# A new order of all steps for a linear-attention and feed-forward kernel on one core

## The chip, the core and the metric

The kernel runs on one core of a Trainium2 chip. A core has TensorE (PE in the profile, its weight loads PEld), VectorE (DVE), ScalarE (ACT), GpSimd (POOL) and SyncE (SP), which here only issues DMA transfers. Each engine works through its own instructions in order and waits for others by semaphores. SBUF holds the operands; PSUM, in eight banks, takes what TensorE produces. The metric is the device time of the program in microseconds.

## The reference

A gated linear recurrence per head, followed by a feed-forward layer on all heads of a token:

```python
# q, k, v, f_logit: (batch 4, heads 8, seq 768, head_dim 48)
f = 1.0 / (1.0 + np.exp(-f_logit))
state = np.zeros((B, H, D, D))
for t in range(S):
    state = f[:, :, t, :, None] * state + np.einsum('bhd,bhe->bhde', k[:, :, t], v[:, :, t])
    y[:, :, t] = np.einsum('bhd,bhde->bhe', q[:, :, t], state)
x = y.transpose(0, 2, 1, 3).reshape(B * S, H * D)      # 3072 x 384
h = x @ w_in                                           # 384 x 2048
out = (h * np.cos(h)) @ w_out                          # 2048 x 384
```

## The kernel before

The 3072 tokens are cut into 12 **pairs** of 256 tokens (`pair(n)`), three for each batch entry; a pair has two chunks of 128 tokens, and the recurrence is written as products of matrices within a chunk plus a carried state. The feed-forward part (`moe(m)`) goes over 13 **units**: units 0 and 1 are the two halves of pair 0 (128 tokens each), and unit m from 2 on is pair m - 1 (256 tokens).

A **step** is a named piece of work of one engine, made of one instruction or a few. Steps of pair n, where u or g after the dot is the half of the heads or the chunk:

- `f`, `k`, `q`, `v`: loads (L296). Pairs 0 and 1 load `f`, `k` and `q` in two halves of 192 KB; the others are whole, 384 KB. `f0.0` or `f0.1` may go by ScalarE's queue.
- `ex`, `ln`, `fx`, `fy` (ScalarE, L329 to L347): the exponential, the softplus and the gate. `ad` (GpSimd, L363) adds two tokens' values. `cum` (TensorE, L374 and L380) sums along time; `eb` and `ei` (ScalarE, L391, L395) take the exponentials of the sums.
- `qa`, `ka`, `qm`, `km` (L338 to L351, L404): q and k scaled, on GpSimd, or in pairs 0 and 1 some on VectorE. `vb`, `vt`: v cast and copied, on GpSimd or ScalarE.
- `tq`, `tk` (L435): transposes on TensorE, copied out of PSUM by `qkt`; for pairs 5 to 11 ("turned") `tq` is a transposing DMA on SyncE's queue instead (L424).
- `sc` (TensorE, L456): scores; `am` (VectorE, L461): their mask. `ps` (TensorE, L479): the new state; `st` and `sz` (VectorE, L497, L503): carrying and decaying it. `y` and `yi` (TensorE, L531): the output within the chunk and from the state. `xe` (ScalarE or VectorE, L197): the output copied to SBUF as the feed-forward part's input.

Steps of unit m: `h` (TensorE, L579): a half of 1024 columns of the first product; `co` (ScalarE, L584): the cosine, by the sine function; `g` (VectorE, L561): h times the cosine. `o` (TensorE, L595, named by the block of 128 tokens): a quarter of the second product; `ot` (ScalarE or VectorE, L197): its copy; `out`: the store. `w` and `wc`: the load of a quarter of a weight matrix, and its cast (L197). All copies have line 197, since one helper writes them.

`zf` (TensorE, L264) is a product of zeros, 128 x 512, into a PSUM bank of its own choice; no result uses it. `z...` of other names clear parts of buffers once.

What sets the order: `describe` builds all steps with what they read and write, and `emit` writes them out in the order of one long string, `ORDER`. A word such as `am1.0:V2` says: step `am1.0`, on VectorE (T TensorE, S ScalarE, V VectorE, G GpSimd, Y SyncE), with its result in place 2 of its pool; where no number stands, the step writes into a value whose place is given already. So the string fixes each engine's queue, the engine of the steps that may choose, and every buffer's place, and with the places who waits for whom: a step that takes a place waits for all readers of what was there. For PSUM the places are the banks 0 to 7; `h` and `sc` take two neighbouring banks, the others one. `apart` releases two steps from each other where they use different banks of one PSUM tile.

On ScalarE the exponential and the sine need different tables; `emit` marks the changes to the first (L637), and a change costs an `ACT_TABLE_LOAD`.

Of the kernel before, what the change touches and what calls it, by code (L numbers as in the profile page):

```python
# [717 lines left out]
```

## Time and profile before

| | |
|---|---|
| time, median of 3 runs (lowest to highest) | 183.1 us (182.93 to 183.41) |
| span of the profiled execution, first to last instruction | 180.9 us |
| around the span, by the median | 2.2 us |
| granted TensorE clock, mean | 1.000 |
| TensorE's last product ends | 177.61 us |
| moved by DMA | 33.93 MB, mean 188 GB/s |

The profile shows one execution. A row of a timeline has the start and the length in us, the engine, the line, what is written and read, and how many instructions are merged in it; in brackets stands how long the engine was idle before, and what ended that. Lengths of merged rows run from the first start to the last end, and neighbouring instructions of an engine overlap by a little. TensorE's products are pipelined: the time from start to start is what a product costs in a row of them.

### The profile page before, as it was taken

To read this page: it belongs to the slowest core of one execution; us is meant where nothing else is said; L and a number is where in the kernel's file an instruction comes from. 1 tells how busy PE (TensorE), PEld (TensorE's weight loads), DVE (VectorE), ACT (ScalarE), POOL (GpSimd) and SP (SyncE) were. 2 spreads that over 40 slices of the span, in tenths; PEclk is the share of its full clock that TensorE was granted. 3 is DMA by queue.
4 is the path that set the end of the run, shared out by engine and by line. 5 is a ranking of instruction groups with operands and counts; after the bars stand their busy time and mean duration, and the time that the engine had idled before them with its cause. 6 is when DMAs were issued, how large, how long until landed. Compare 5 with 4: busy or idle time off the path is not lost.

```text
span 180.9 us, 5814 instructions
## 1 busy us (share of the span) xinstructions
PE 172.6 (95%) x2460; PEld 123.9 (69%) x2464; DVE 134.6 (74%) x206; ACT 130.7 (72%) x187; POOL 109.2 (60%) x139
## 2 busy tenths in 40 slices
...
GB/s 149 261 261 276 343 320 341 250 318 284 301 265 233 274 83 123 252 210 145 122 180 308 173 267 278 124 131 251 203 92 182 100 4 0 43 47 4 130 43 131
DMA packets 72282, 33.93 MB, mean 188 GB/s; under 512 B 65344, under 2 KB 70720, under 8 KB 72256
## 3 DMA queue, kind: packets, MB, share of 16 engines
...
## 4 chain that ended last, share of the span: by engine, by line
PE 81%; DMA 7%; ACT 3%; DVE 3%; SPq 2%; issue 1%; ACTq 0%
PE ps L595 35%; PE ps L579 33%; PE ps L531 5%; DMA f<-in_f_logit_dram 4%; PE ps L456 4%; DMA v<-in_v_dram 3%; SPq L296 2%; PE ps L479 2%; DVE g L561 1%; PE ps L435 1%; PE ps L374 1%; DVE am L461 1%; PE ps L264 1%; ACT f L344 0%; ACT f L329 0%
## 5 line engine op out<-in xcount | busy, mean ns | idle before, releaser
L561 DVE TENSOR_TENSOR g<-ps,co 128x1024 bf16<-128x1024 f32 x48 | 57.4, 1220 | 18.0 <-ACT co L584 16.7
L595 PE MATMUL ps<-w_out_bf,g 128*128 128x384 bf16 x384 | 68.9, 326 | 0.0
L579 PE MATMUL ps<-x,w_in_bf 128*128 128x256 bf16 (+1 forms) x624 | 68.1, 264 | 0.5 <-DVE x L197 0.4
L584 ACT ACTIVATE co<-ps,halfpi 128x1024 bf16<-128x1024 f32 x48 | 52.7, 1113 | 19.8 <-PE ps L579 19.5
L579 PEld LDWEIGHTS <-w_in_bf 128*128 128x128 bf16 x624 | 56.3, 98 | 9.2 <-DVE x L197 0.6
L595 PEld LDWEIGHTS <-g 128*128 128x128 bf16 x384 | 36.1, 98 | 21.4
L461 DVE TENSOR_TENSOR am<-ps,pmask 128x1024 bf16<-128x1024 f32 x24 | 28.7, 1218 | 5.2 <-PE ps L456 4.9
L404 POOL TENSOR_TENSOR qk<-k,bi 128x384 bf16<-128x384 f32 x22 | 22.0, 1008 | 5.4 <-ACT bi L391 4.7
L404 POOL TENSOR_TENSOR qk<-q,b 128x384 bf16<-128x384 f32 x21 | 20.8, 1000 | 2.7 <-DVE q L338 2.1
L197 POOL COPY vt<-vb 64x384 bf16<-64x384 bf16 x33 | 16.7, 507 | 1.6
L264 PE MATMUL ps<-zero 128*128 128x512 bf16 x50 | 14.6, 412 | 1.5 <-DVE zero L203 1.2
L503 DVE TENSOR_TENSOR sz<-ps,b 64x192 bf16<-64x192 f32 x40 | 14.1, 354 | 2.5 <-PE ps L479 1.6
L363 POOL TENSOR_TENSOR sp<-ls 128x384 bf16<-128x384 f32 x10 | 10.3, 1028 | 7.8 <-ACT ls L333 6.1
L341 POOL TENSOR_TENSOR q<-f,q 128x384 f32<-128x384 f32 x10 | 10.0, 998 | 8.0 <-DMA q<-in_q_dram 5.8
L329 ACT ACTIVATE f<-f 128x768 f32<-128x768 f32 (+1 forms) x14 | 10.4, 746 | 4.4 <-DMA f<-in_f_logit_dram 4.4
L497 DVE TENSOR_TENSOR ps<-ps,sz 64x192 f32<-64x192 f32 x32 | 11.7, 367 | 2.2 <-PE ps L479 1.1
L351 POOL TENSOR_TENSOR k<-k,f 128x384 f32<-128x384 f32 (+1 forms) x12 | 11.1, 931 | 3.4 <-DMA k<-in_k_dram 3.4
L197 ACT COPY ot<-ps 128x384 f32<-128x384 f32 (+1 forms) x14 | 6.1, 453 | 8.7 <-PE ps L595 8.7
L197 ACT CAST x<-ps 128x384 bf16<-128x384 f32 x12 | 5.5, 479 | 6.0 <-PE ps L531 6.0
L456 PE MATMUL ps<-qkt 48*64 48x128 bf16 (+1 forms) x304 | 8.7, 218 | 1.1 <-ACT x L197 0.8
L197 DVE CAST x<-ps 128x384 bf16<-128x384 f32 x12 | 6.4, 553 | 4.1 <-PE ps L531 3.9
L264 PEld LDWEIGHTS <-zero 128*128 128x128 bf16 x54 | 4.8, 103 | 5.9 <-issue 1.9
...
## 6 DMA issues: line engine op xcount, KB each, us to landing
...
```

The lines of the kernel that those rows point to most:

```text
L197: (nc.scalar.copy if e == "ACT" else eng(e).tensor_copy)(out=o, in_=i)
L264: G.step(f"zf{i}", ("PE",), lambda e, dump=dump: nc.tensor.matmul(dump.ap, lhsT=zero[:, 0:128], rhs=zero, start=True, stop=True), writes=[ ...
L351: eng(e).tensor_mul(out=w.ap[:, :, 0, :], in0=w.ap[:, :, 0, :], in1=t.ap[:, :, 0, :])
L404: G.step(f"{nm}{n}.{u}", ("POOL", "DVE") if cut else ("POOL",), lambda e, u=u, j=j, src=src, dec=dec: eng(e).tensor_mul(out=qkp[u][j].ap[: ...
L456: nc.tensor.matmul(o[t0:t1, r, 2 * a + g, :].rearrange("p (e n) -> p e n", e=2), lhsT=wide[s, t0 // 64, :] if turned else wide[s].rearrang ...
L461: G.step(f"am{n}.{u}", ("DVE",), lambda e, u=u, sc=sc: nc.vector.tensor_mul(out=am[u].ap.rearrange("p r b n -> p (r b) n"), in0=sc.ap.rear ...
L497: nc.vector.tensor_add(out=view()[s], in0=view()[s], in1=S0.ap[s, :, r, :])
L503: eng(e).tensor_mul(out=new.ap[s, :, r, :].rearrange("p (u a) n -> p u a n", u=2), in0=view()[s].rearrange("p (u a) n -> p u a n", u=2), i ...
L561: nc.vector.tensor_mul(out=o.rearrange("p b (n e) -> p b n e", e=2), in0=ph.ap.rearrange("p (b e n) -> p b n e", e=2, n=64), in1=co.ap.rea ...
L579: nc.tensor.matmul(ph.ap[:, i * T:(i + 1) * T].rearrange("p (g t) -> p g t", t=C), lhsT=w_in_bf[:, kk, f0:f0 + 128], rhs=xa[:, :, kk, :], ...
L584: G.step(f"co{m}.{j}", ("ACT",), lambda e, ph=ph, co=co: nc.scalar.activation(out=co.ap, in_=ph.ap, func=AF.Sin, bias=halfpi), reads=[ph], ...
L595: nc.tensor.matmul(po.ap[:, 0:DM], lhsT=gT.ap[:, j, i * C:(i + 1) * C], rhs=w_out_bf[:, j, :], start=(po.first and j == 4 * s), stop=(po.f ...
```

## The change

`ORDER` is replaced as a whole: all 899 steps other than the zero products stand in a new sequence; engines and places are chosen anew; and there are 58 zero products instead of 54. The steps themselves, their shapes and their number are the same, and so are the pools.

Counted over the two strings: `xe` goes from 12 on ScalarE and 12 on VectorE to 8 and 16, `ot` from 14 and 12 to 10 and 16; `vb` from 9 on GpSimd and 3 on ScalarE to 8 and 4; of the scalings of pairs 0 and 1, `qm` has one more and `km` one less on VectorE. One more of the last stores goes by ScalarE's queue. But for the clears, the other choices keep their numbers. ScalarE's queue changes between the two tables 10 times before (5 to the sine, 5 back) and 12 times after.

TensorE's first feed-forward step is `h0.01` before, between parts of pair 1; after, it is `h1.00`, behind all of pairs 0 and 1. The weights are loaded in the order `w0.1 w0.0 w0.3 w0.2 w1.0 w1.2 w1.3 w1.1` before and `w0.0 w0.2 w0.1 w0.3 w1.2 w1.1 w1.3 w1.0` after.

The beginning and the end of both strings:

```diff
 WITHIN = 12
-ZEROS = 54
+ZEROS = 58
...
 ORDER = """
-zvt.2:V zsp.1:V zsp.0:G zsz.3:V f0.1:Y0 f0.0:S zqk.0:G k0.0:Y0 ex0.1:S ex0.0:S k0.1:Y ln0.1:S1
-zf0:T0 zf1:T0 zf2:T0 zf3:T0 zf4:T0 zf5:T0 zf6:T0 zf7:T0 zf8:T0 zf9:T0 cum0.1:T0 ln0.0:S cum0.0:T1
-fx0.0:S ei0.1:S0 fx0.1:S ei0.0:S ka0.0:V f1.1:Y1 km0.0:G0 f1.0:Y ex1.1:S ka0.1:V zf10:T2 zf11:T2
-zf12:T2 zf13:T2 zf14:T2 zf15:T2 zf16:T2 zf17:T2 tk0.0:T2 eb0.1:S0 ex1.0:S ln1.1:S1 ln1.0:S fx1.0:S
-q0.1:Y0 q0.0:Y v0:Y0 fx1.1:S eb0.0:S qa0.1:V zqk.1:V qm0.1:V vb0:S0 f3:Y2 k1.1:Y1 km0.1:V qa0.0:V
-zf18:T3 cum1.1:T3 zf19:T4 zf20:T4 zf21:T4 tq0.1:T0 cum1.0:T1 qm0.0:G zsz.2:G eb1.0:S1 vt0.3:S2
-k1.0:Y ei1.0:S0 ex3:S zf22:T4 zf23:T4 zf24:T4 zf25:T4 zf26:T4 ps0.1:T4,5 ps0.0:T tk0.1:T v1:Y1 f2:Y0
-qkt0.1:V0 eb1.1:S ln3:S0 ei1.1:S ka1.0:G q1.0:Y0 tq0.0:T ka1.1:G km1.1:G0 zvt.1:G vt0.0:S ad3:G1
-vt0.1:G q1.1:Y vb1:S1 qkt0.0:V1 vt0.2:G zsz.1:G ex2:S w0.1:Y0 w0.0:Y1 k3:Y0 q3:Y1 w0.3:Y2 ln2:S1
-vt1.2:S1 fy3:S zf27:T6 zf28:T6 zf29:T6 zf30:T6 zf31:T6 zf32:T6 sc0.0:T0 sz0.01:V2 sz0.00:V w0.2:Y3
-ad2:G0 vt1.0:G km1.0:V vt1.3:G wc0.1:G am0.0:V0 zf33:T6 zf34:T6 yi0:T4 sc0.1:T2 am0.1:V1 st0.11:V
-sz0.11:V3 wc0.0:G k2:Y1 zf35:T6 zf36:T6 zf37:T6 zf38:T6 ps1.1:T6,7 tk1.0:T0 ps1.0:T zf39:T1 zf40:T1
-zf41:T1 cum3:T1 fy2:S ei3:S0 fx3:S ka3:G eb3:S2 vt1.1:S fx2:S km3.0:G1 qa3:G qm3.0:G km3.1:G qm3.1:G
-w1.0:Y0 qa1.0:V st0.10:V qa1.1:V qm1.0:V wc0.2:G ka2:G q2:Y2 tk1.1:T2 zf42:T3 zf43:T3 y0:T3 tq1.0:T
-xe0.1:S0 sz0.10:V st1.00:V st1.01:V qm1.1:V v2:Y1 zf44:T5 zf45:T5 zf46:T5 zf47:T5 zf48:T5 tq1.1:T
-cum2:T1 sz1.00:V1 qkt1.0:V0 eb2:S0 xe0.0:S ei2:S1 qkt1.1:V1 km2.0:G0 km2.1:G zf49:T5 sc1.0:T4
-sz1.01:V zf50:T0 zf51:T0 sc1.1:T2 h0.01:T0 st1.11:V sz1.11:V2 am1.1:V0 wc1.0:G qa2:G zf52:T6 zf53:T6
-h0.00:T co0.0:S0 qm2.1:G am1.0:V1 h1.01:T2 h1.00:T co1.0:S1 y1:T6,4 yi1:T g0.0:V1 xe1.1:V1 st1.10:V
-qm2.0:G vb2:G1 sz1.10:V g1.0:V4 w1.2:Y3 xe1.0:S tk3.0:T5 h2.01:T0 tq3.0:T w1.3:Y0 qkt3.0:V0 v3:Y0
-f4:Y0 h2.10:T6 h2.00:T sc3.0:T4 tq3.1:T2 tk3.1:T h2.11:T wc1.2:G wc1.3:G vt2.1:G1 wc0.3:S vb3:G0
-co2.0:S1 am3.0:V0 g2.0:V2 h2.20:T4 h2.21:T h0.11:T0 co2.1:S0 qkt3.1:S1 co2.2:S1 sc3.1:T2 w1.1:Y3
-g2.1:V am3.1:V1 g2.2:V h0.10:T h1.11:T6 h1.10:T h2.30:T2 tk2.1:T4 tk2.0:T5 co0.1:S0 co1.1:S2 g0.1:V
-g1.1:V h2.31:T o2.0:T0 co2.3:S0 tq2.1:T vt3.2:G2 vt3.1:G tq2.0:T o0.0:T1 o3.0:T6 o1.0:T7 qkt2.0:S2
...
-o22.1:T3 o22.2:T out16:Y o20.3:T6 o20.0:T g11.1:V o20.1:T h12.01:T o20.2:T co12.0:S0 g12.0:V o21.2:T
-o22.3:T o21.1:T o23.3:T7 o22.0:T ot20:V3 ot21:V1 out20:Y ot22.0:V2 ot22.1:V out22.0:Y out21:Y
-out22.1:Y o23.2:T o23.0:T o23.1:T ot23.0:S3 out23.0:Y ot23.1:S out23.1:S
+zqk.2:G k0.1:Y1 zqk.0:G zsz.0:V zvt.0:V f0.0:S1 zsp.0:V ex0.0:S f0.1:Y ex0.1:S ln0.1:S0 fx0.1:S
+ln0.0:S f1.1:Y2 ex1.1:S zf0:T0 zf1:T0 zf2:T0 zf3:T0 zf4:T0 zf5:T0 zf6:T0 zf7:T0 zf8:T0 zf9:T0
+zf10:T0 zf11:T0 zf12:T0 zf13:T0 zf14:T0 zf15:T0 zf16:T0 cum0.1:T4 fx0.0:S ei0.1:S0 zf17:T5 zf18:T5
+cum0.0:T2 eb0.0:S1 eb0.1:S ln1.1:S0 ei0.0:S zf19:T0 zf20:T0 zf21:T0 zf22:T0 zf23:T0 zf24:T0
+cum1.1:T1 q0.0:Y0 zsz.3:V q0.1:Y qa0.1:V qa0.0:V qm0.0:V2 k0.0:Y ka0.0:V km0.0:G zvt.2:G v0:Y1
+f1.0:Y k1.1:Y2 vb0:S0 fx1.1:S ka0.1:V km0.1:V vt0.3:G0 vt0.1:S zsp.1:G zf25:T0 zf26:T0 zf27:T0
+zf28:T0 zf29:T0 zf30:T0 ps0.1:T2,7 ei1.1:S1 ps0.0:T qm0.1:V tk0.1:T4 sz0.01:V0 sz0.00:V zqk.1:V
+st0.11:V zsz.1:G tq0.1:T tq0.0:T3 zsz.2:G eb1.1:S0 tk0.0:T qkt0.1:V0 zf31:T6 zf32:T6 zf33:T6 zf34:T6
+sc0.1:T4 ex1.0:S qkt0.0:S1 yi0:T6 sz0.11:V1 st0.10:V q1.1:Y2 qa1.1:V qm1.1:V2 sz0.10:V ln1.0:S
+sc0.0:T0 cum1.0:T2 eb1.0:S vt0.2:G ka1.1:G km1.1:G v1:Y2 zf35:T3 tk1.1:T3 q1.0:Y fx1.0:S qa1.0:V
+am0.1:V0 vb1:G1 qm1.0:V am0.0:V3 tq1.1:T qkt1.1:S1 zf36:T7 zf37:T7 zf38:T7 zf39:T7 zf40:T7 zf41:T7
+sc1.1:T4 am1.1:V1 vt1.3:S2 vt1.1:S vt0.0:G zf42:T7 zf43:T7 zf44:T7 zf45:T7 zf46:T7 y0:T3 k1.0:Y
+ei1.0:S ka1.0:G km1.0:G vt1.0:G tk1.0:T0 tq1.0:T ps1.0:T7,5 ps1.1:T qkt1.0:V0 st1.00:V sz1.00:V0
+st1.01:V sz1.01:V f3:Y0 ex3:S ln3:S1 ad3:G1 zf47:T2 sc1.0:T0 am1.0:V2 f2:Y1 ex2:S xe0.0:V0 ln2:S0
+fx3:S fy2:S ad2:G0 zf48:T2 zf49:T2 zf50:T2 zf51:T2 zf52:T2 zf53:T2 zf54:T2 zf55:T2 cum2:T2 xe0.1:V
+cum3:T4 ei2:S0 ei3:S1 eb2:S1 eb3:S2 fx2:S st1.10:V fy3:S zvt.1:V yi1:T1,7 vt1.2:G y1:T xe1.1:V1
+w0.0:Y3 wc0.0:G zf56:T0 h1.00:T2 xe1.0:V h2.01:T6 h2.00:T st1.11:V sz1.11:V3 sz1.10:V w0.2:Y0
+wc0.2:G h0.00:T4 w0.1:Y4 co2.0:S0 wc0.1:G h0.01:T co0.0:S3 h1.01:T g2.0:V2 g0.0:V4 co1.0:S0 g1.0:V0
+h2.21:T0 h2.20:T co2.2:S1 g2.2:V k3:Y1 ka3:G km3.1:G0 h0.10:T6 w0.3:Y1 wc0.3:G h0.11:T co0.1:S3
+g0.1:V v3:Y0 vb3:G2 vt3.1:S1 h2.11:T4 h2.10:T co2.1:S0 h2.31:T2 km3.0:G ps3.0:T0,1 ps3.1:T sz3.00:V2
+sz3.01:V g2.1:V q3:Y2 tk3.0:T6 qa3:G qm3.0:G tk3.1:T7 tq3.0:T h2.30:T vt3.3:S zf57:T0 h1.11:T4
+qm3.1:G w1.2:Y3 vt3.0:G wc1.2:S qkt3.0:V2 tq3.1:T st3.10:V q2:Y1 qa2:G st3.11:V h1.10:T o2.2:T0
+sz3.10:V0 co2.3:S0 g2.3:V qkt3.1:S3 sc3.0:T6 sz3.11:V sc3.1:T2 qm2.0:G1 qm2.1:G vt3.2:G o3.2:T1
+w1.1:Y1 wc1.1:S am3.0:V0 o2.1:T am3.1:V2 k2:Y0 o3.1:T ka2:G km2.0:G o1.1:T6 co1.1:S3 tq2.0:T7 f5:Y2
+ex5:S g1.1:V tk2.0:T yi3:T2 y3:T3 qkt2.0:V0 xe3.0:S3 xe3.1:V tq2.1:T5 km2.1:G tk2.1:T o1.2:T w1.3:Y3
+wc1.3:G ln5:S1 sc2.0:T2 qkt2.1:V2 sc2.1:T4 ad5:G0 o3.3:T am2.1:V3 v2:Y0 vb2:S0 fy5:S o2.3:T am2.0:V1
+zsp.2:V ps2.0:T5 ps2.1:T st2.00:V st2.01:V f4:Y1 ex4:S ln4:S0 fx4:S fx5:S cum5:T7 ei5:S0 fy4:S
+o1.3:T vt2.1:G0 eb5:S0 vt2.0:G vt2.3:G h4.21:T2 h4.20:T sz2.01:V1 sz2.00:V yi2:T4,5 vt2.2:G y2:T
+w1.0:Y1 wc1.0:G o1.0:T xe2.0:V2 xe2.1:V ot1:V3 f6:Y0 ex6:S ad4:G1 cum4:T7 ei4:S1 eb4:S2 o3.0:T
+ot3:V0 k5:Y2 ka5:G o2.0:T ot2:V1 co4.2:S2 g4.2:V3 km5.0:G1 h3.31:T4 h3.30:T h3.01:T0 h3.00:T
+h4.10:T6 co3.3:S0 g3.3:V1 h4.11:T q5:Y1 co3.0:S1 g3.0:V k4:Y0 qa5:G ka4:G km4.1:G2 h3.21:T2 co4.1:S3
+q4:Y0 qa4:G km4.0:G qm4.0:G qm4.1:G h3.20:T out1:Y v4:Y0 g4.1:V h3.11:T4 h3.10:T vb4:G2 co3.2:S0
+g3.2:V co3.1:S3 g3.1:V h4.31:T0 tk4.1:T7 v5:Y2 vb5:G1 qm5.0:G tq4.0:T6 tk4.0:T h4.30:T co4.3:S0
+tq4.1:T qkt4.1:V4 o5.0:T2 g4.3:V o5.3:T qkt4.0:V1 o0.1:T5 o5.1:T sc4.1:T0 ps4.1:T3,4 ps4.0:T
+st4.01:V st4.00:V sz4.01:V2 sz4.00:V sc4.0:T6 am4.0:V0 o0.3:T o5.2:T o0.0:T vt5.3:G2 vt4.0:G1
+qm5.1:G km5.1:G ln6:S0 vt4.3:G ad6:G2 cum6:T3 o0.2:T o4.3:T6 f7:Y2 ex7:S ln7:S1 fx7:S vt5.0:G
+vt4.1:G ad7:G2 k6:Y0 f8:Y1 o4.1:T out3:Y tq5.0:Y3 v6:Y1 q7:Y1 st4.11:V ot5:V3 am4.1:V2 st4.10:V
+vt5.1:S fy6:S eb6:S1 ex8:S sz4.11:V1 yi4:T7,2 ln8:S1 ps5.0:T0 ps5.1:T sz4.10:V st5.01:V vt4.2:G y4:T
+xe4.0:V2 ot0:V2 st5.00:V sz5.00:V3 sz5.01:V xe4.1:V fy7:S fx6:S cum7:T1 eb7:S2 ei7:S1 ei6:S2 fx8:S
+o4.2:T o4.0:T ot4:S0 h4.01:T4 h4.00:T co4.0:S3 tq5.1:Y0 sc5.0:T0 am5.0:V2 sc5.1:T6 am5.1:V1 h5.20:T2
...
+h11.30:T co11.3:S1 g11.3:V o18.1:T o18.2:T h12.31:T4 o20.1:T7 h12.10:T2 h12.11:T out17:Y out19:Y
+ot18:V1 out16:Y out12:Y out18:Y h12.01:T0 h12.00:T co12.1:S3 co12.0:S2 g12.0:V g12.1:V o21.2:T6
+o20.2:T o21.3:T o21.0:T o20.3:T h12.30:T co12.3:S3 o22.1:T0 o21.1:T o20.0:T o22.2:T o22.0:T g12.3:V
+o22.3:T o23.0:T4 ot22.1:V1 o23.2:T ot22.0:S out22.0:S ot21:V2 out21:Y ot20:V0 out22.1:Y out20:Y
+o23.1:T o23.3:T ot23.0:V3 ot23.1:S out23.1:Y out23.0:S
 """
```

90 lines of the change are left out of this document (36 added, 54 removed).

## The prediction

> **What bounds the kernel now.** I read the page's first part, then busy times by stretch, then TensorE's own timeline.
>
> ```profile
> span 180.9 us, 5814 instructions
> PE 172.6 (95%) x2460; PEld 123.9 (69%) x2464; DVE 134.6 (74%) x206; ACT 130.7 (72%) x187; POOL 109.2 (60%) x139
> 1.19:4.88 3.69, 3.69 (x10) 1.32 (x11) 2.36 (x16) 1.88 (x3) 1.26 (x5) 1.00 0.84 207
> 4.88:23.57 18.69, 15.56 (x226) 8.71 (x230) 13.29 (x28) 15.73 (x37) 11.35 (x15) 1.00 1.20 286
> 23.57:33.92 10.35, 9.68 (x172) 7.62 (x172) 8.65 (x13) 7.55 (x10) 10.11 (x11) 1.00 1.09 330
> 33.92:177.61 143.69, 143.67 (x2052) 106.28 (x2051) 110.02 (x149) 105.01 (x138) 85.89 (x105) 1.00 0.71 167
> ```
>
> The stretches give start:end and length, then busy time of TensorE, its weight loads, VectorE, ScalarE and GpSimd, then the granted clock, the DMA share and GB/s. From 33.92 to 177.61 us TensorE is busy 143.67 of 143.69 us: a new order can gain nothing there, only lose. What there is to win lies before 33.92. There TensorE is busy 3.69 + 15.56 + 9.68 = 28.93 of 32.73 us, 3.80 idle, and part of the busy time is products of zeros, 54 in the program. After TensorE's end only 3.3 us are left.
>
> TensorE's timeline names the idle time (in brackets: idle before the row, and what ended it):
>
> ```profile
> 1.19 3.69 PE L264 MATMUL ps<-zero 128*128 128x512 bf16 x10 [1.19 <-DVE zero L203]
> 5.68 0.33 PE L374 MATMUL ps<-sp,incl 128*128 128x192 bf16 x2 [0.81 <-ACT sp L333]
> 6.36 1.89 PE L264 MATMUL ps<-zero 128*128 128x512 bf16 x8
> 8.50 0.38 PE L264 MATMUL ps<-zero 128*128 128x512 bf16 x1
> 17.26 0.59 PE L264 MATMUL ps<-zero 128*128 128x512 bf16 x2 [0.16 <-issue]
> 20.08 0.40 PE L435 MATMUL ps<-ident,qk 128*128 128x128 bf16 x4 [0.74 <-DVE qk L404]
> 21.81 0.40 PE L435 MATMUL ps<-ident,qk 128*128 128x128 bf16 x4 [0.23 <-DVE qk L404]
> 23.57 0.40 PE L456 MATMUL ps<-qkt 48*128 48x128 bf16 x8 [0.78 <-ACT x L197]
> 29.70 0.83 PE L579 MATMUL ps<-x,w_in_bf 128*128 128x256 bf16 x6 [0.42 <-DVE x L197]
> ```
>
> Named waits: 0.81 + 0.16 + 0.74 + 0.23 + 0.78 + 0.42 = 3.14 us; the other 0.66 is spread thin, and I keep it. So the end of TensorE is 1.19 + real work + zeros + waits, and I cost the change on these terms.
>
> **Real work.** Both orders hold the same 298 real steps of TensorE. What differs is how often TensorE changes the shape of its tile, which the chain shows:
>
> ```profile
> 40.95 0.45 PE ps L435 x8
> 54.12 0.65 PE ps L595 x4
> 71.75 0.90 PE ps L531 x56
> 72.64 0.76 PE ps L595 x4
> ```
>
> Four products of the second layer take 0.65 us between others of full shape and 0.76 straight after the 32-column products of L531: 0.1 us per change. I counted the neighbours of different shape in the lists (full; `ps` and turned `sc`; unturned `sc`; `y`/`yi`): 69 before, 67 after. That is -0.2 us.
>
> **Zeros.** Eight in a row take 1.89 us, so (1.89 - 0.38) / 7 = 0.216 each (0.38 is one alone, as at 8.50). Four more: +0.86 us. They cost only because they stand in front of real steps; where a wait stood there anyway they cost nothing, so the bounds are 0 and 0.86. I take 0.86 here and count the waits of the new order behind its zeros, so that nothing counts twice.
>
> **Waits of the new order.** Loads first. When a load lands I take from its place in the issue order, since the queues are full (DMA share over 1) and the rows below show landing in order.
>
> ```profile
> 4.28 0.94 ACT L329 ACTIVATE f<-f 128x384 f32<-128x384 f32 x2 [1.76 <-DMA f<-in_f_logit_dram]
> 8.41 0.36 DVE L338 SCALAR_TENSOR_TENSOR q<-f,q 128x192 f32<-128x192 f32 x1 [1.12 <-DMA q<-in_q_dram]
> 10.67 0.83 ACT L197 CAST vb<-v 128x768 bf16<-128x768 f32 x1 [0.79 <-DMA v<-in_v_dram]
> 17.71 0.84 ACT L329 ACTIVATE f<-f 128x768 f32<-128x768 f32 x1 [1.73 <-DMA f<-in_f_logit_dram]
> ```
>
> In half loads (192 KB) these are the 1st, 7th, 10th and 18th: 4.3, 8.4, 10.6 and 17.7 us. In the new order `f0.1` is 3rd (5.4 us by interpolation, against 4.3: `k0.1` now goes ahead of it), `q0.1` 6th (7.7), `v0` 9th (9.9), and `f2` 20th (18.9).
>
> Then VectorE's queue, whose prices are these groups (mean ns after the bar):
>
> ```profile
> L561 DVE TENSOR_TENSOR g<-ps,co 128x1024 bf16<-128x1024 f32 x48 | 57.4, 1220 | 18.0 <-ACT co L584 16.7 <-issue 0.6
> L584 ACT ACTIVATE co<-ps,halfpi 128x1024 bf16<-128x1024 f32 x48 | 52.7, 1113 | 19.8 <-PE ps L579 19.5
> L503 DVE TENSOR_TENSOR sz<-ps,b 64x192 bf16<-64x192 f32 x40 | 14.1, 354 | 2.5 <-PE ps L479 1.6
> L497 DVE TENSOR_TENSOR ps<-ps,sz 64x192 f32<-64x192 f32 x32 | 11.7, 367 | 2.2 <-PE ps L479 1.1
> L197 DVE COPY qkt<-ps 128x1024 bf16<-128x1024 bf16 x7 | 4.6, 681 | 2.9 <-PE ps L435 2.9
> L404 DVE TENSOR_TENSOR qk<-q,b 128x384 bf16<-128x384 f32 x3 | 1.6, 533 | 0.0
> L338 DVE SCALAR_TENSOR_TENSOR q<-f,q 128x192 f32<-128x192 f32 x4 | 1.6, 392 | 1.1 <-DMA q<-in_q_dram 1.1
> 24.95 2.36 DVE L461 TENSOR_TENSOR am<-ps,pmask 128x1024 bf16<-128x1024 f32 x2 [0.43 <-PE ps L456]
> 56.15 1.02 DVE L197 CAST x<-ps 128x384 bf16<-128x384 f32 x2 [1.97 <-PE ps L531]
> 8.78 0.27 DVE L231 MEMSET qk<- 128x256 uint32 x1
> ```
>
> - *`ps0.1`*: 17 zeros end at 4.88 + 7 x 0.216 = 6.4; three `cum` steps (0.35 each, by the rows at 5.68 and 6.36) and 14 zeros bring TensorE to 10.5. It needs `vb0`: 9.9 + 0.83 = 10.75. Wait 0.2. `ps0` ends at 11.4.
> - *`sc0.1`*: VectorE does two `sz`, a memset, `st0.11` and `qkt0.1`: 0.71 + 0.27 + 0.37 + 0.68 = 2.03, to 13.45. TensorE, with four transposing steps (0.22 each, by L435 x8) and four zeros, is free at 13.1. Wait 0.4.
> - *`y0`*: VectorE goes on with two `sz`, `st`, two `qa`, two `qm`, `am0.1`, `am0.0`: 5.3, to 18.7. TensorE has, after 13.5, 12 zeros (2.6), three `sc` (1.0, by the row at 23.57) and `yi0`, `cum1.0`, two transposes (1.0), to 18.1. Wait 0.6.
> - *`h2.01`* needs `xe1.1` and `xe1.0`, the last of VectorE's next 12 instructions: `am1.1`, `qkt1.0`, four `st`/`sz`, `am1.0`, two `xe`, `st`, memset, two `xe` = 7.2, to 25.9. TensorE's own list in that time (ten zeros 2.2, `y0`, `yi1` and `y1` 1.5 by L531 x56, `h1.00` 0.7, transposes, `ps`, `sc` and two `cum` 1.8) ends at 25.05. Wait 0.85.
> - *`h0.11`* needs `wc0.3`. 7.47 MB are ordered up to `w0.3`. By 23.57 us 207 x 3.69 + 286 x 18.69 = 6.1 MB have moved, and at 330 GB/s the rest takes 4.1 us, to 27.7. Neighbouring transfers overlap, so I say 29 to 30. GpSimd has `wc0.1`, two products of 1 us and the cast of 1.47 in a row, to 31.5. TensorE is there at 31.2. Wait 0.3.
> - *`tk3.0`*, *`h1.11`*, *`sc3.1`* each take PSUM banks that a gate product on VectorE must release. `g0.1`: 32.2 + 1.11 + 1.22, to 34.6 (TensorE 34.4). `g2.1`, behind two `sz`, at 36.6 (36.2). `g2.3`, behind `qkt3.0` and three small ones, at 39.5 (39.2). Waits 0.2 + 0.4 + 0.3.
>
> ```profile
> L404 POOL TENSOR_TENSOR qk<-k,bi 128x384 bf16<-128x384 f32 x22 | 22.0, 1008 | 5.4 <-ACT bi L391 4.7
> L197 POOL CAST w_in_bf<-g 128x1536 bf16<-128x1536 f32 x3 | 4.3, 1465 | 0.1
> ```
>
> Together 3.25 against 3.14: +0.1. From `yi2` on I followed the queues with the same prices and found TensorE always the last to arrive, though often by only 0.2 to 0.5 us. The SyncE queue is reordered too: `out1` and `out6` now stand ahead of loads and transposes, but what is behind them is needed 3 us or more after its landing. I cost the rest at nothing; the cover is TensorE's own backlog of `o` steps, and each 0.3 us of wrong price above that would be paid in full.
>
> **Tail.** Both halves of `ot23` were on ScalarE; now one is on VectorE.
>
> ```profile
> 177.63 0.54 ACT L197 COPY ot<-ps 128x192 f32<-128x192 f32 x2 [4.74 <-PE ps L595]
> 178.20 0.36 ACTq L606 DMA_DIRECT2D out_dram<-ot  x1
> L197 DVE COPY ot<-ps 128x192 f32<-128x192 f32 x2 | 0.6, 353 | 0.6 <-PE ps L595 0.6
> ```
>
> The last transfer can go at 177.63 + 0.35 instead of 178.20: -0.2 us. It is one transfer's latency either way.
>
> **The sum.** -0.2 + 0.86 + 0.1 - 0.2 = +0.56 on the span of 180.9; the median of the runs (183.1) lies 2.2 above that, and I take that distance as it is: 183.6 us. Bounds: all waits of the list gone, and zeros free: -3.5; the trace has nothing that excludes it, but the landing rows speak against it.
>
> **A rule against the trace.** The first ten zeros take 3.69 us, the eight at 6.36 only 1.89, while the granted clock reads 1.00 in every stretch: products start at half pace and go to full pace some 3.4 us in. *The Trainium skill, "TensorE: Matmul & The Clock Gate", Part 1: The HAM clock gate, says that the array's clock is halved until it has been busy for a window of about 3.4 us and again after an idle window; the pace of the zeros agrees, the clock column doesn't show it. By that rule 17 zeros in a row at the start add nothing to the warm-up, and waits as short as those above leave the clock alone, so my sum is the same.* The way in which it would not be the same is a rival below.
>
> **The rivals.**
> - *The start is quicker than my list.* Each wait there is under 0.9 us and stands on rounded prices. If VectorE is 5% quicker or the weights land at 27.7, `ps0.1`, `h0.11`, `tk3.0`, `h1.11`, `sc3.1` and half of `sc0.1` don't wait: 3.25 - 1.6 = 1.65, so 182.0 us. For: the row of two `am` (2.36) shows that neighbours overlap. Against: no row has a hop between engines for nothing.
> - *Weights land late (the other side).* From `h0.11` on VectorE works without a pause up to `sz2.00`, so each microsecond by which `wc0.3` ends after 31.2 goes to `g0.1`, `g2.1`, `g2.3` and into TensorE.
>
> ```profile
> DMA to landing us min/median/max: 5.1/7.1/10.0
> ```
>
> These are the weights' own transfers: the slowest needs 2.9 us more than the median. It decides from a landing after 30 us on; with half of the spread, +1.5: 185.1 us.
> - *ScalarE starves TensorE later.* The list changes between the exponential and the sine six times where the old one did it five times.
>
> ```profile
> L584 ACT ACT_TABLE_LOAD x5 | 6.4, 1283 | 0.1
> ```
>
> That is 2 x 1.28 = 2.6 us more, and while `ln6` to `ot4` run (16 instructions) no `co` frees a PSUM pair. TensorE has 12 `o` steps for that time, so I think it is covered; uncovered, 186.2 us.
> - *The clock falls.* If a pause sums up with others so that TensorE goes to half pace again for 3.4 us, 1.7 us are lost: 185.3 us. *This is the page's rule about idle windows.* Pauses of 0.81 and 0.78 us did not do it before.
>
> **How the numbers follow.** The forecast has 0.45 (182.7 to 184.4), the quick start 0.26, late weights 0.15, ScalarE 0.10, the clock 0.04. 0.3% (0.55 us) is about what a measurement of this kernel tells from no change. The forecast's own range reaches over that bound: 0.19 of it is within, 0.25 slower, 0.01 faster; the quick start is faster but for 0.02. So faster 0.25, within 0.21, slower 0.54. The range 181.6 to 186.0 leaves out a start without any wait and the worst end of the ScalarE case.
>
> **What would show it.** Right: TensorE's waits before 40 us sum to 3 to 4 us, the largest ahead of the first 256-wide L579, near 25.9 and ended by DVE `x`; no idle TensorE later; the last `out` issue 0.4 us after TensorE's end. Wrong: idle time of TensorE after 55 us, zeros at 0.43 us after the first 4 us, or L579 waiting for GpSimd's `w_in_bf`.

## The result, and the profile after

The changed kernel takes 185.2 us (median of four runs, 184.03 to 187.3) against 183.0 us before (182.38 to 183.41); the ratio is 1.0101, interval 1.0059 to 1.0142. It is slower, by about 2.2 us. The runs of the new order lie much further apart than those of the old one, so the ratio here and those below leave out runs more than 1.5% above the fastest of their kernel, while medians and lowest and highest times are of all runs.

The profiled execution took 185.59 us, with a span of 183.8 us, 2.9 us more than before. The new kernel's lines stand one further down (the first product is L580, the second L596; in most kernels of the experiments L581 and L597). The first lines of its page:

```profile
span 183.8 us, 5827 instructions
PE 174.6 (95%) x2468; PEld 125.3 (68%) x2468; DVE 140.5 (76%) x216; ACT 131.2 (71%) x182; POOL 107.6 (59%) x136
```

TensorE's busy time rose by 2.0 us, and VectorE works 5.9 us more. Of the 2.0 us, four more zeros account for 0.86, and 0.44 is gaps in the record of before, which lacks four zeros (it lists `L264` x50 of the 54, and 2460 products for 2464 weight loads). Where TensorE loses time shows in the stretches (start:end and length; TensorE, its weight loads, VectorE, ScalarE, GpSimd; granted clock; DMA share; GB/s):

```profile
0.00:42.00 42.00, 37.32 (x535) 24.79 (x536) 33.74 (x71) 32.83 (x53) 30.48 (x44) 1.00 1.07 278
42.00:98.00 56.00, 55.95 (x829) 40.97 (x826) 48.97 (x71) 51.49 (x70) 45.45 (x54) 1.00 0.98 224
98.00:124.00 26.00, 25.38 (x394) 18.49 (x393) 19.97 (x30) 22.47 (x33) 18.32 (x22) 1.00 1.01 210
```

Before, TensorE had no idle time from 33.92 us to its end. Now 0.62 us are missing between 98 and 124 us. TensorE's own timeline names the waits (in brackets):

```profile
7.02 0.32 PE L375 MATMUL ps<-sp,incl 128*128 128x192 bf16 x2 [0.70 <-ACT sp L334]
11.54 0.44 PE L480 MATMUL ps<-vb,qk 64*64 64x48 bf16 x32 [0.26 <-ACT f L348]
14.30 0.40 PE L457 MATMUL ps<-qkt 48*128 48x128 bf16 x8 [0.46 <-DVE qkt L198]
16.97 0.40 PE L436 MATMUL ps<-ident,qk 128*128 128x128 bf16 x4 [0.85 <-DVE qk L405]
27.62 4.57 PE L580 MATMUL ps<-x,w_in_bf 128*128 128x256 bf16 x58 [0.39 <-DVE x L198]
36.34 0.83 PE L436 MATMUL ps<-ident,qk 128*128 128x128 bf16 x12 [0.26 <-DVE g L562]
38.23 0.83 PE L580 MATMUL ps<-x,w_in_bf 128*128 128x128 bf16 x12 [0.19 <-DVE g L562]
41.14 0.40 PE L457 MATMUL ps<-qkt 48*128 48x128 bf16 x8 [0.17 <-DVE g L562]
99.58 0.41 PE L532 MATMUL ps<-am,vt 128*32 128x128 bf16 x16 [0.36 <-POOL vt L198]
102.47 2.79 PE L580 MATMUL ps<-x,w_in_bf 128*128 128x256 bf16 x24 [0.26 <-DVE ot L198]
```

The eight waits before 42 us sum to 3.28 us. The two at 99.58 and 102.47 us are new. TensorE's last row ends its work at 173.32 + 6.66 = 179.98 us instead of 177.61, and 3.8 us are left after it instead of 3.3:

```profile
173.32 6.66 PE L596 MATMUL ps<-w_out_bf,g 128*128 128x384 bf16 x40
```

### The profile page after: what moved, and what is told of

Same layout as the page of the kernel before. It is cut to its first block, busy times and chain, and to the rows that moved or that the text cites. A ratio compares the mean times of both kernels' runs of the same rounds, so it can differ in the third digit from the quotient of the medians.

```text
span 183.8 us, 5827 instructions
## 1 busy us (share of the span) xinstructions
PE 174.6 (95%) x2468; PEld 125.3 (68%) x2468; DVE 140.5 (76%) x216; ACT 131.2 (71%) x182; POOL 107.6 (59%) x136
## 2 busy tenths in 40 slices
DMA packets 72281, 33.92 MB, mean 185 GB/s; under 512 B 65344, under 2 KB 70720, under 8 KB 72256
## 4 chain that ended last, share of the span: by engine, by line
PE 55%; DVE 13%; DMA 9%; POOL 7%; SPq 6%; issue 4%; ACT 3%; DVEq 0%; POOLq 0%
PE ps L580 23%; PE ps L596 23%; DMA v<-in_v_dram 6%; POOL qk L405 4%; PE ps L532 4%; SPq L297 4%; DVE g L562 3%; SPq L425 3%; DMA out_dram<-ot 3%; DVE sz L504 2%; PE ps L457 2%; DVE am L462 2%; DVE ps L498 2%; PE ps L436 1%; POOL sp L364 1%
## 5 line engine op out<-in xcount | busy, mean ns | idle before, releaser
L580 PE MATMUL ps<-x,w_in_bf 128*128 128x256 bf16 (+1 forms) x624 | 67.9, 264 | 0.8 <-DVE x L198 0.4
L596 PE MATMUL ps<-w_out_bf,g 128*128 128x384 bf16 x384 | 68.7, 326 | 0.0
L580 PEld LDWEIGHTS <-w_in_bf 128*128 128x128 bf16 x624 | 56.6, 98 | 10.1 <-issue 1.2
L596 PEld LDWEIGHTS <-g 128*128 128x128 bf16 x384 | 36.0, 98 | 21.4
L405 POOL TENSOR_TENSOR qk<-k,bi 128x384 bf16<-128x384 f32 x23 | 23.0, 1000 | 10.7 <-DVE k L352 7.2
L405 POOL TENSOR_TENSOR qk<-q,b 128x384 bf16<-128x384 f32 x20 | 19.6, 1000 | 0.3
L265 PE MATMUL ps<-zero 128*128 128x512 bf16 x58 | 15.8, 406 | 1.2 <-DVE zero L204 1.2
L198 DVE COPY ot<-ps 128x384 f32<-128x384 f32 (+1 forms) x16 | 8.2, 527 | 4.2 <-PE ps L596 3.0
L198 DVE CAST x<-ps 128x384 bf16<-128x384 f32 x16 | 8.5, 549 | 3.5 <-PE ps L532 3.5
L198 ACT CAST x<-ps 128x384 bf16<-128x384 f32 x8 | 3.7, 478 | 9.3 <-PE ps L532 9.2
L265 PEld LDWEIGHTS <-zero 128*128 128x128 bf16 x58 | 5.5, 103 | 7.0 <-issue 1.7
```

Of the source, the lines that this page charges most:

```text
L198: (nc.scalar.copy if e == "ACT" else eng(e).tensor_copy)(out=o, in_=i)
L265: G.step(f"zf{i}", ("PE",), lambda e, dump=dump: nc.tensor.matmul(dump.ap, lhsT=zero[:, 0:128], rhs=zero, start=True, stop=True), writes=[ ...
L405: G.step(f"{nm}{n}.{u}", ("POOL", "DVE") if cut else ("POOL",), lambda e, u=u, j=j, src=src, dec=dec: eng(e).tensor_mul(out=qkp[u][j].ap[: ...
L580: nc.tensor.matmul(ph.ap[:, i * T:(i + 1) * T].rearrange("p (g t) -> p g t", t=C), lhsT=w_in_bf[:, kk, f0:f0 + 128], rhs=xa[:, :, kk, :], ...
L596: nc.tensor.matmul(po.ap[:, 0:DM], lhsT=gT.ap[:, j, i * C:(i + 1) * C], rhs=w_out_bf[:, j, :], start=(po.first and j == 4 * s), stop=(po.f ...
```

## The experiments

The theory after this profile: TensorE is not short of work, but the new order lets it meet VectorE in the start and single transfers near 100 us with hardly any margin, and pays at the end. The rivals: the four more zero products, the granted clock, or an order that is slower everywhere. Each kernel ran beside the one before on the same chip; that one took 183.2 us (medians of 183.22 each time, 182.49 to 184.55 in 58 runs, granted clock 0.997 or more in each).

| run | median us (lowest to highest), runs | ratio to before, interval | granted clocks |
|---|---|---|---|
| a_again | 187.96 (186.25 to 189.18), 6 | 1.0222, 1.0176 to 1.0267 | 0.986 to 1.000 |
| e1_tail | 186.21 (184.29 to 187.33), 6 | 1.0112, 1.0067 to 1.0156 | 0.988 to 1.000 |
| e2_mid | 184.74 (184.09 to 188.38), 10 | 1.0089, 1.0053 to 1.0125 | 0.991 to 1.000 |
| e4_port | 187.02 (184.04 to 189.78), 10 | 1.0101, 1.0064 to 1.0138 | 0.991 to 1.000 |
| e5_place | 186.43 (184.81 to 188.16), 6 | 1.0152, 1.0104 to 1.0199 | 0.991 to 1.000 |
| e3_zeros | 187.37 (184.96 to 189.93), 6 | 1.0178, 1.0131 to 1.0225 | 0.982 to 0.995 |
| e6_all | 185.27 (184.40 to 186.91), 6 | 1.0126, 1.0088 to 1.0165 | 0.998 to 1.000 |
| e7_share | 183.20 (183.04 to 184.49), 12 | 1.0016, 0.9998 to 1.0034 | 0.998 to 1.000 |
| e8_gap | 186.04 (185.51 to 187.35), 6 | 1.0161, 1.0129 to 1.0193 | 0.988 to 1.000 |
| e9_share | 183.19 (182.60 to 183.44), 12 | 0.9995, 0.9984 to 1.0006 | 0.997 to 1.000 |
| e10_bzeros | 184.43 (183.31 to 185.79), 12 | 1.0070, 1.0042 to 1.0097 | 0.980 to 0.989 |
| e11_all | 184.81 (184.35 to 185.84), 6 | 1.0093, 1.0066 to 1.0121 | 0.996 to 1.000 |

### The changed kernel again

> The changed kernel once more, beside which the next three are read. If its lateness is in its order, it stays 1.8 to 2.6 us above the kernel before, TensorE's row sequence again has its waits ahead of the first 256-wide L580 (0.4 us) and near 99 and 102 us (0.4 and 0.3 us), and its runs spread by no more than 1 us. If much of the lateness was chance in the timing of the transfers (its four runs went from 184.0 to 187.3), the waits near 99 and 102 us come and go and the distance to the kernel before falls under 1.5 us.

It ran from 186.25 to 189.18 us: the same program that took 184.0 us once took 189.2 another time. Its distance to before (4.7 us) and its spread (2.9 us) are larger than expected. In its profile the wait near 102 us has grown. First the lines of the changed kernel's profile around that place (chain, ScalarE), then the same of this one (TensorE, VectorE, ScalarE, SyncE's issue):

```profile
96.87 4.90 DMA out_dram<-ot
102.25 1.11 ACT L585 ACTIVATE co<-ps,halfpi 128x1024 bf16<-128x1024 f32 x1 [0.37 <-PE ps L580]
```

```profile
103.19 2.79 PE L581 MATMUL ps<-x,w_in_bf 128*128 128x256 bf16 x24 [1.17 <-ACT co L586]
102.58 0.56 DVE L199 COPY ot<-ps 128x384 f32<-128x384 f32 x1 [1.94 <-DMA out_dram<-ot]
96.83 1.42 SPq L608 DMA_DIRECT2D out_dram<-ot  x1
```

The releaser named is ScalarE's `co`, but in the first profile the same product started at 102.47 us, while that `co` ran until 103.36. What it waits for is the copy `ot7`, which ends at 103.14 here. `ot7` needs a place that the store `out2` still reads. The store took 4.90 us from issue to landing there and about 5.7 here (96.83 to 102.58 at the latest); TensorE waited 0.26 and 1.17 us. The margin is smaller than the spread of one transfer.

### The steps near 100 us moved ahead

```diff
-ad9:G1 ... vt6.3:G ... vt6.2:G        (GpSimd)
+vt6.3:G vt6.2:G ad9:G1 ...
-tq6.0:Y0 ... out2:Y                   (SyncE)
+out2:Y tq6.0:Y0 ...
```

> Two queues change near 90 to 100 us: vt6.3 and vt6.2 go ahead of ad9 on GpSimd, and out2 goes ahead of the transpose tq6.0 on SyncE. Theory: y6 waits for vt6.2 (0.36 us), which stands behind ad9, which waits 5.8 us for ScalarE; and h7.2 waits for ot7, which waits for the store of out2, which stands behind three transposes. With both gone TensorE's end comes 0.8 to 1.1 us earlier, and the run is as much faster than a_again. Rival: TensorE is held by ScalarE's cosines right behind (table load at 100.6, first cosine at 102.25), so a new wait takes the place of the old ones and the gain is under 0.4 us.

No wait of TensorE over 0.2 us is left after 60 us. The one that remains:

```profile
PE ps L458 <- DMA qkt<-qk: 0.2, 1, 0.2
```

The profiled execution has a span of 182.5 us, 1.3 us under that of the changed kernel. Of this, 0.6 us is an earlier start (`h2.01` at 27.00 instead of 27.62 us), which these moves don't touch; 0.5 us is won from there to TensorE's end (151.8 instead of 152.4 us), where the two waits of 0.62 us were. So what was lost between 98 and 108 us is the order of those three steps: `vt6.2`, which `y6` needs, stood behind `ad9`, and `out2` behind three transposes in SyncE's queue. But four of the ten runs still took 186.18 us or more, so this is not the whole spread.

### The tail

```diff
-ot23.0:V3 ot23.1:S out23.1:Y out23.0:S
+ot23.0:S3 out23.0:Y ot23.1:S out23.1:S
```

> Only the last stores change: both halves of ot23 on ScalarE again, their stores as in the kernel before. Theory: in the changed kernel ScalarE's half waits for VectorE's half (its row starts at 180.41, after VectorE's ends at 180.38), so the split costs where it was meant to save; undoing it makes the time from TensorE's end to the end of the span 3.3 us instead of 3.8 and the run 0.3 to 0.5 us faster than a_again. Rival: the tail is longer only because the last transfers take longer to land; then nothing moves by more than 0.2 us.

The last two copies and stores go as they did before, and the tail is as long as in the changed kernel: from the end of TensorE's last row (175.17 + 6.66 = 181.83) to the span's end (185.6) are 3.8 us.

```profile
175.17 6.66 PE L597 MATMUL ps<-w_out_bf,g 128*128 128x384 bf16 x40
```

The changed place of `ot23.0` costs nothing. What differs from before at the end is the closing wait of SyncE for TensorE's sequencer (total, times, longest): first before, then the changed kernel.

```profile
SPq L713 <- PEq L713: 0.6, 2, 0.4
```

```profile
SPq L714 <- PEq L714: 1.0, 2, 0.9
```

It is 0.7 to 0.9 us in all profiles of the new order and 0.4 in those of the old one, and only the new ones have a transfer of instructions (0.01 MB) near the span's end. Why TensorE's program ends later I did not test; this part of the 0.5 us stays open.

The profiled execution, one of the long ones (187.33 us), holds another wait:

```profile
112.33 2.78 PE L581 MATMUL ps<-x,w_in_bf 128*128 128x256 bf16 x24 [2.24 <-ACT x L199]
104.74 0.37 SPq L298 DMA_DIRECT2D v<-in_v_dram  x1
110.06 0.83 ACT L199 CAST vb<-v 128x768 bf16<-128x768 f32 x1 [2.86 <-DMA v<-in_v_dram]
111.81 0.47 ACT L199 CAST x<-ps 128x384 bf16<-128x384 f32 x1
```

`v9` shares place 1 with `v8`, so it is issued only when `vb8` is done, at 104.74 us. It lands 5.3 us later; its cast `vb9` stands on ScalarE ahead of `co7.1` and `xe7.1`, and TensorE's next product waits 2.24 us for the latter. In the first profile of the changed kernel `v9` was issued at 104.64 and landed by 108.21:

```profile
108.21 0.83 ACT L198 CAST vb<-v 128x768 bf16<-128x768 f32 x1 [0.54 <-DMA v<-in_v_dram]
```

Same issue, 1.8 us between the landings, and a wait of 0 or 2.24 us on TensorE. The profile of the next section (189.35 us) has this wait too; that the other long runs have it is likely, but they have no profile.

### VectorE next to GpSimd

```diff
-vb1:G1 ... vt0.0:G ... k1.0:Y ... ka1.0:G
+vb1:S1 ... k1.0:Y ka1.0:G vt0.0:G
```

> In the start vb1 is cast by ScalarE instead of GpSimd, and GpSimd does vt0.0 after ka1.0. So GpSimd is free while VectorE does qm1.1. Theory: VectorE's products of two SBUF operands slow down while GpSimd works (qm1.1 took 0.99 us and km0.1 about 0.7 to 1.2, where 0.53 is usual): qm1.1 falls to 0.5 to 0.6 us, qa1.1 (still beside km1.1) stays near 0.76, the first 256-wide L580 starts 0.3 to 0.5 us earlier, and the run is 0.2 to 0.5 us faster. Rival: they are late for their operands, not slow: qm1.1 keeps its 0.9 to 1.0 us, and the run is the same, or up to 0.4 us slower because ScalarE has 0.8 us more ahead of qkt1.1.

Of the start, three instructions of VectorE and three of GpSimd in the changed kernel, then VectorE's last two in this one:

```profile
10.14 1.26 DVE L405 TENSOR_TENSOR qk<-k,bi 128x384 bf16<-128x384 f32 x1
15.06 0.76 DVE L339 SCALAR_TENSOR_TENSOR q<-f,q 128x192 f32<-128x192 f32 x1
15.92 0.99 DVE L405 TENSOR_TENSOR qk<-q,b 128x384 bf16<-128x384 f32 x1
9.98 1.00 POOL L405 TENSOR_TENSOR qk<-k,bi 128x384 bf16<-128x384 f32 x1 [7.23 <-DVE k L352]
14.60 1.00 POOL L405 TENSOR_TENSOR qk<-k,bi 128x384 bf16<-128x384 f32 x1
15.55 0.95 POOL L198 CAST vb<-v 128x768 bf16<-128x768 f32 x1
```

```profile
14.51 0.76 DVE L340 SCALAR_TENSOR_TENSOR q<-f,q 128x192 f32<-128x192 f32 x1
15.37 0.56 DVE L406 TENSOR_TENSOR qk<-q,b 128x384 bf16<-128x384 f32 x1
```

With `vb1` gone from GpSimd, `qm1.1` falls from 0.99 to 0.56 us; `qa1.1`, beside which GpSimd still has `km1.1`, stays at 0.76 against 0.39 in the mean of before. In the changed kernel each of the three ends 0.2 to 0.4 us after the instruction of GpSimd beside it (11.40 after 10.98, 15.82 after 15.60, 16.91 after 16.50), whenever it began. The profile of before has the same thing: its two `km` on VectorE take 738 ns in the mean, one 0.55 us alone at 9.38 us, the other 0.93 us beside GpSimd's `k`, which end at 14.87 us:

```profile
14.36 0.93 DVE L404 TENSOR_TENSOR qk<-k,bi 128x384 bf16<-128x384 f32 x1
```

*The Trainium skill, "SBUF — State Buffer", section "SBUF: two separate sides", says that VectorE and GpSimd share one pair of ports, that an instruction of VectorE with two inputs in SBUF needs it against one of GpSimd that reads SBUF, and that the later one is blocked fully. The rows agree, as far as four cases go; only `qm1.1` was tested by taking its neighbour away.* The gain reaches TensorE: its first product on `h2.01` starts 15.65 us after `ps0.1` instead of 16.08 (and 15.67 in the first kernel with all repairs). But the times of this kernel did not fall: its profile has the wait for `vb9` (2.29 us) and behind it a clock at half:

```profile
112.00:114.00 2.00, 1.28 (x12) 1.15 (x12) 1.60 (x2) 1.95 (x5) 1.86 (x4) 1.00 0.94 117
114.00:116.00 2.00, 2.00 (x12) 1.43 (x11) 1.65 (x4) 1.97 (x3) 0.37 (x1) 0.51 0.99 271
```

### The places of the v loads

```diff
-v7:Y1 ... v9:Y1 ... v10:Y2
+v7:Y2 ... v9:Y2 ... v10:Y1
```

> Only the places of three v loads are changed in the new order: v7 and v9 take place 2 and v10 place 1, so that no v load waits for the cast of the one just before it. Theory (thin margin on a transfer): in the slow profiles v9 is issued at 104.7 to 105.1 us, because it shares place 1 with v8, and TensorE then waits 2.2 to 2.3 us near 112. With place 2 it is issued near 99.5 us, right behind out9, lands near 105, and the wait near 112 goes; the runs then end between 184.0 and 186 and the highest stays under 187 (before this edit 184.0 to 189.8), the median about 184.8. What is left of the spread is out2's store near 100 us. Rival (the spread is the granted clock or the chip, not this load): highest again 188 to 190, median 186 to 188, as in the repeat of the changed kernel.

`v9` is issued at 101.28 us instead of 104.7, although this profile runs 1.5 us behind the others by then, and no wait of TensorE near 112 us is left.

```profile
101.28 0.44 SPq L298 DMA_DIRECT2D v<-in_v_dram  x1
```

The runs are not closer together, though, and the profiled one (188.16 us) shows why: its clock halves in the start.

```profile
14.00:16.00 2.00, 1.54 (x37) 1.07 (x37) 1.90 (x4) 0.75 (x3) 1.84 (x4) 1.00 1.31 266
16.00:18.00 2.00, 1.15 (x10) 0.73 (x10) 1.90 (x5) 0.71 (x3) 2.00 (x3) 0.83 1.16 295
18.00:20.00 2.00, 2.00 (x6) 0.59 (x4) 2.00 (x3) 1.95 (x4) 0.28 (x1) 0.50 1.05 386
20.00:22.00 2.00, 2.00 (x18) 0.77 (x17) 1.66 (x2) 1.94 (x4) 1.44 (x2) 0.82 1.04 385
```

By these clocks it is at half for 0.68 + 2.00 + 0.72 = 3.40 us and takes 1.70 us of TensorE's pace, which is a mean clock of 0.991 over 186 us; 1.28 us of it reach `h2.01`, which starts 17.36 us after `ps0.1` instead of 16.08. It sets in after the pauses of 0.46 and 0.85 us ahead of `sc0.1` and `tq1.1`, which the first profile has as well, without a fall. Of the 32 runs with the start of the new order unchanged 7 have a mean clock of 0.991 or less; of the 58 runs of before, none. *The Trainium skill, "TensorE: Matmul & The Clock Gate", Part 1: The HAM clock gate, speaks of a free-running window of 3.4 us, so that the same work falls differently into it from run to run; the 3.40 us and the runs agree. It names an idle window as what halves the clock; the profile differs, and decides here: TensorE was busy 1.54 and 1.15 of 2 us.* `out2`'s store took longer still in this profile and cost TensorE 1.45 us besides:

```profile
98.37 5.98 DMA out_dram<-ot
105.06 2.79 PE L581 MATMUL ps<-x,w_in_bf 128*128 128x256 bf16 x24 [1.45 <-DVE ot L199]
```

### Fewer zero products, in the new order and in the old

```diff
-ZEROS = 58    (zf47 to zf57 left out of the order)
+ZEROS = 47
```

> The last 11 of the 58 zero products (those near 21 to 30 us) are left out; nothing else changes. Theory of the prediction's term: each stands in the way of real products at 0.21 us, so 11 cost 2.4 us of TensorE time, of which only what lies on the path comes back: the lowest run falls from 184.0 to 182.5 to 183.5. Rival (VectorE and GpSimd set the start, the zeros lie in TensorE's waiting time): first 256-wide product of L581 again at 25.4 to 26.0 us and the lowest run 183.8 to 184.3. Rival (the zeros hold the clock up): granted clock lower than 1.0 in the first 40 us, or products twice as long there, and a time 1 to 3 us longer.

All six runs have a clock under 1 (0.982 to 0.995), and the lowest is 184.96 us. Dropping 11 products that take 2.4 us gained nothing: TensorE's first product on `h2.01` starts at 29.19 us, against 29.16 in the kernel of the section above, and VectorE does the mask `am1.0` at the same time as there. That profile has the same early fall of the clock, and all 58 zeros; first this kernel, then that one.

```profile
25.41 1.22 DVE L462 TENSOR_TENSOR am<-ps,pmask 128x1024 bf16<-128x1024 f32 x1
```

```profile
25.38 1.22 DVE L463 TENSOR_TENSOR am<-ps,pmask 128x1024 bf16<-128x1024 f32 x1
```

TensorE waits where the zeros were, and a second fall of the clock follows:

```profile
26.68 0.52 PE L532 MATMUL ps<-qkt,sz 128*32 128x128 bf16 x24 [1.31 <-DVE am L462]
28.00:30.00 2.00, 1.96 (x16) 1.53 (x15) 1.92 (x6) 1.25 (x1) 2.00 (x3) 0.50 0.98 219
```

The same cut in the kernel before:

```diff
-ZEROS = 54    (zf42 to zf53 left out of the order)
+ZEROS = 42
```

> The kernel before without its last 12 of 54 zero products (those between 19 and 27 us). Theory (the zeros lie in TensorE's waiting time and hold the granted clock up): VectorE's times up to 24 us as before, the clock falls to half for 3 us once or twice in most runs, mean clock 0.982 to 0.993, median 184.5 to 187. Rival (each zero stands in the way of real products): 12 times 0.21 is 2.5 us less TensorE work, median 181 to 182.5. Rival (they neither cost nor help): 182.9 to 183.5, clock 0.997 to 1.0.

All 12 runs have a clock of 0.980 to 0.989, where none of before is under 0.997, and the median rises by 1.2 us. Its stretches:

```profile
22.00:24.00 2.00, 0.90 (x15) 0.61 (x14) 1.94 (x5) 1.96 (x6) 1.93 (x2) 0.99 1.26 288
24.00:26.00 2.00, 1.67 (x19) 1.47 (x19) 1.33 (x3) 1.96 (x3) 1.92 (x3) 0.50 1.08 339
```

So these last zeros stand in TensorE's waiting time and hold the clock up. They are not the cost of the change; the zeros ahead of them were not tested.

### Zeros in the pause

```diff
-tq1.1:T
+zf:T7 zf:T7 zf:T7 zf:T7 tq1.1:T      (ZEROS = 62)
```

on top of the moves near 100 us and the places of the v loads.

> The new order with the places of the v loads changed, vt6.3 and vt6.2 ahead of ad9, out2 ahead of tq6.0, and four more zero products (62) in TensorE's pause ahead of tq1.1 near 16 us. Theory (a pause of 0.85 us there, behind one of 0.46 us, is what lets the granted clock halve for 3.3 us in some runs, at 1.7 us each): no run has a mean granted clock under 0.996, and the four zeros cost nothing, because VectorE sets the start; first 256-wide product as late as without them, runs 184.0 to 185.5. Rival (the clock falls at moments that have nothing to do with this pause): clocks of 0.991 in one or two of the runs as in the four kernels with this pause before, and 186 to 188 us in these. Rival (each zero costs its 0.21 us): lowest run 0.8 us above that of the same kernel without them, 184.9.

This kernel does not answer the question: the bank that I chose was still held for VectorE's `sz`, so the zeros waited too, and the pause stayed.

```profile
16.77 1.02 PE L266 MATMUL ps<-zero 128*128 128x512 bf16 x4 [1.11 <-DVE sz L505]
```

One run of six fell to 0.988, and the lowest run is 185.51 us. `h2.01` starts 17.18 us after `ps0.1` instead of 16.08. So the four zeros cost 1.1 us: they have to find a free bank to fill a pause.

### A shared place in the kernel before

```diff
-v9:Y1
+v9:Y0
```

> The kernel before, with one place changed: v9 goes to place 0, which v8 holds, as the new order does it. Theory: v9's issue moves from 94.95 us to the end of vb8, 102.2, and holds k9 and the transposes behind it in SyncE's queue; it lands near 107.5, so vb9 on GpSimd moves from 103.1 to about 107.5, and with it the q and k rows of block 9; TensorE waits 1 to 4 us near 108 to 116, the median rises from 183.2 to 184.5 to 187, and the runs spread by 1.5 us or more where they spread by 0.6. Rival (the load has 8 us of slack in any order, the spread belongs to the order as a whole): 183.0 to 183.6 as before, no spread.

In this order `v9` stands ahead of the cast that reads `v8`, so no wait came about: block 8 is computed with `v9`'s data, and the time says nothing on the question. The next kernel moves the load behind `vb8` as well.

> The kernel before, with the v load of block 9 put into the place of block 8 and, as that asks for, moved in the order to behind the cast vb8. Theory (what the new order has near 105 us: a load that waits for the cast of the load just before it): v9 is issued at about 102.5 instead of 95 to 96 us, lands 5 to 6 us later, vb9 on GpSimd moves from 103.1 to about 108, and TensorE waits 1 to 4 us between 108 and 120; median 184.5 to 187, spread 1 us or more. Rival (before has enough slack behind vb9, its next reader being a transpose near 111 and TensorE at 114): 183.0 to 183.8 as before.

The rival holds. `v9` goes out at 102.37 us and `vb9` moves by 3 us:

```profile
102.37 0.37 SPq L298 DMA_DIRECT2D v<-in_v_dram  x1
106.09 0.82 POOL L199 CAST vb<-v 128x768 bf16<-128x768 f32 x1 [2.78 <-DMA v<-in_v_dram]
```

The median is 183.19 us. Here the shared place costs nothing: in the old order the next steps that read `vb9` come at 113 us, and no step that TensorE needs at once stands behind its cast. In the new order `xe7.1` does.

### All repairs together

First without zeros in the pause, then with two ahead of `tq1.1`, each with the moves near 100 us, the places of the v loads and `vb1` on ScalarE.

> Four repairs of the new order together: vt6.3 and vt6.2 ahead of ad9 on GpSimd, out2's store ahead of the transpose tq6.0 on SyncE, the v places of the run beside it, and at the start vb1 on ScalarE with vt0.0 moved behind ka1.0. Theory: no wait of TensorE over 0.3 us is left between 60 and 120 us, the runs lie close together (lowest 183.3 to 183.8, highest under 185.5), median 183.8, that is within 0.3 to 0.5% of before: what is left is 0.4 us of later start, 0.5 us of tail and the zeros. Rival (the spread has another cause): lowest 183.5, highest 188 or more.

> All repairs at once: those of the first kernel beside it with two zeros in place of four ahead of tq1.1, and vb1 on ScalarE with vt0.0 behind ka1.0, which takes GpSimd away from beside VectorE's qm1.1. Theory: qm1.1 0.55 us instead of 0.99, TensorE's pause ahead of tq1.1 under 0.1 us, no wait over 0.5 us from 60 us on, no clock under 0.997; lowest run 183.4 to 184.0, highest under 185.3, median about 184.2, so still 0.3 to 0.6% over before: VectorE's start and 0.5 us at the end are left. Rival (another engine or the transfers now set the pace): no lower than the kernel beside it.

Of these 12 runs none has a clock under 0.996, and they lie within 184.35 to 186.91 us, where the unrepaired order reached 189.18. But the lowest runs, 184.40 and 184.35, are 0.3 to 0.6 us above what was expected, and the first profile still waits 0.57 us for a transpose by DMA near 94 us. In the second TensorE works through from 98 to 124 us, where it waited; but its two zeros wait for the same bank as in the section on the pause, and its first product of 256 columns on `h2.01` is about as late as ever:

```profile
16.35 0.59 PE L266 MATMUL ps<-zero 128*128 128x512 bf16 x2 [0.68 <-DVE sz L505]
27.42 8.09 PE L581 MATMUL ps<-x,w_in_bf 128*128 128x256 bf16 x102 [0.39 <-DVE x L199]
98.00:124.00 26.00, 26.00 (x419) 19.43 (x422) 20.70 (x30) 22.61 (x33) 16.34 (x20) 1.00 0.90 202
```

`h2.01` starts 16.32 us after `ps0.1` here and 15.67 in the first of the two, so the zeros took back what moving `vb1` had won. The kernel is still 0.9% slower than before (1.0066 to 1.0121), with a span of 182.6 us against 180.9: TensorE ends 1.1 us later (178.75), and the tail is 0.5 us longer. I found no version of the new order that beats the old one.

## Why the prediction was right or wrong

The sign and the range held: 183.6 us was forecast, 181.6 to 186.0 with slower the likeliest, and 185.2 was measured. But the sum of +0.56 us stands against +2.9 in the profiled execution, and much of the hit is luck. 185.2 lies outside what the forecast itself was given (182.7 to 184.4); late weights and ScalarE, the rivals that carried the range so far up, did not come. And without the zeros' 0.86 us, which the runs with fewer zeros do not bear out, the sum would have been -0.30, faster.

Of the 2.3 us that the sum lacks, 1.6 are in TensorE's end (178.37 by the sum, 179.98 measured) and 0.7 in the tail. `h2.01` starts at 27.62 us instead of 25.9; from there to TensorE's end the profile has 152.4 us and the sum 152.5. So in this execution the start is the whole of TensorE's part. Term by term:

- **Real work and waits of the start.** The sum of the waits looked good, 3.25 forecast and 3.28 measured, by luck: the walk behind it failed in two places, here and in the next item, and its later waits came out shorter (0.62 instead of 1.2 us), which hid this in the sum. The first place is before `ps0.1`, which starts at 11.54 us instead of 10.75. `f0.1` lands near 5.9 us, not 5.4, and `cum0.1` waits 0.70 us for ScalarE's softplus, a wait that the walk does not have; with it TensorE itself is free only at 11.29. From `y0` to `h2.01` the walk's 7.2 us were right. The term of -0.2 for changes of shape was not tested.
- **VectorE's price list.** This is the second place: `km0.1`, `qa1.1` and `qm1.1` took 1.26, 0.76 and 0.99 us where I took 0.53, 0.39 and 0.53, because GpSimd read SBUF at the same time. Of `km0.1`'s 0.73 us at most 0.25 reach TensorE, which was late already; the other two, 0.8 us, stand in the way from `sc0.1` to `y0` (6.06 us instead of 5.2). This is shown for `qm1.1` by the run that took `vb1` away; for the other two it rests on their rows. The profile of before had the row to see it, the `km` of 0.93 us; the price list has only the faster `qm`.
- **Idle time spread thin, 0.66, kept.** Of this and of the 0.16 us ahead of 17.26, 0.44 us are the gaps where four zeros are missing from the record of before: work, and no wait.
- **Zeros, +0.86.** Mis-sized: 0 for those that were tested. Both runs without the last zeros show them in waiting time that VectorE sets. The bound of 0 was in the text; I chose the wrong end.
- **From `yi2` on, nothing.** In the first profile this step is wrong by 0.62 us of named waits, which the shorter waits before them happen to balance; in the long runs it failed most, with 1.45 us at `out2` alone in another profile, from three moved steps, and 2.2 us when `v9` lands late. The text said that TensorE is the last to arrive "often by only 0.2 to 0.5 us", and that the SyncE queue leaves 3 us behind `out1` and `out6`; it did not follow `out2` and `v9`, whose landings alone differ by 1.1 and 1.8 us from run to run. A margin must be held against the spread of what it waits for, not against zero.
- **Tail, -0.2.** Measured +0.5. The halves on two engines are not the cause, as the tail run shows; the closing wait for TensorE's sequencer is longer by 0.5 us (0.9 against 0.4), for a reason left open.

The rivals: the weights did not land late, and no wait after ScalarE's table loads shows. The clock does fall to a mean of 0.991 or less in 7 of 32 runs where I gave 0.04, and at 1.7 us of pace, of which 1.28 reached `h2.01`, close to the price given; it is a second reason why the runs spread, and pauses about as short as those of before were enough. Of "what would show it", the waits before 40 us came out at 3 to 4 us (by the luck named above), but the largest is ahead of `tq1.1` and not of `h2.01`, and TensorE does idle after 55 us.
